# Wider dummy matmuls, fewer of them, and another order of the work

## The chip, the cores and the metric

The kernel runs on one core of a Trainium2 chip. A core has engines that each work through a queue of their own, in order: TensorE (PE in the profile; its weight loads are listed apart as PEld), VectorE (DVE), ScalarE (ACT), GpSimd (POOL) and SyncE (SP), which here only issues transfers. SBUF is the core's working memory; matmuls write to PSUM, here eight banks of 128 x 512 floats. The metric is the device time of one execution in microseconds (us), as a median over several runs.

## The reference

Eight sequences of 448 tokens with 12 heads of 64 go through an attention whose queries and keys are normalised, and then through a feed-forward layer of 768 to 2048 to 768 with a hard swish. There is no causal mask.

```python
def rmsnorm(x, g):
    return x / sqrt(mean(x * x, axis=-1) + 1e-6) * g
# q, k, v: (8, 12, 448, 64)
q_n, k_n = rmsnorm(q, g_q), rmsnorm(k, g_k)
scores = (q_n @ k_n.T) / sqrt(64)
attn = softmax(scores) @ v
x = attn.transpose(0, 2, 1, 3).reshape(3584, 768)
h = x @ w_in                      # (3584, 2048)
g = h * clip(h + 3, 0, 6) / 6
out = g @ w_out                   # (3584, 768)
```

## The kernel before

**Units of work.** Two heads of one sequence make a pair P; there are 48 pairs, six to a sequence (a batch b). For each pair SyncE loads q, k and v (256 KB each). The squares of q and k are taken on GpSimd or ScalarE (`square`, lines 357 to 361), summed over 64 on VectorE (L446, L480), and turned into inverse roots by a logarithm and an exponential on ScalarE (`roots`, L422 and L425). GpSimd or VectorE scales q and k by these to bf16 (`scale`, L364), and a cast brings v to bf16 beside a column of ones (`values`, by `copy`, L343 to L349). Pairs under 13 are transposed by TensorE into PSUM (L534) and copied out; later pairs by a transfer on SyncE's queue (L553), with a scaling behind it (L561, L563).

**Scores and weighted sums.** TensorE takes the scores of 112 keys against all 448 queries for both heads (L586, two matmuls that use 64 rows of the array each); ScalarE makes their exponentials (L592). The exponentials are the stationary operand of the weighted sums over v (L672), where the column of ones gives the sum for the softmax; VectorE divides (L688, L691). The result is transposed to xT by TensorE in batches 0 and 1 (L707, copied out), later by SyncE (L698).

**Feed-forward.** For each batch, 16 groups of hidden units: six matmuls of 448 columns into a PSUM bank (L764), then a clipped ReLU on ScalarE (L723) and one multiplication on VectorE (L726). For two batches together, 7 tiles of output rows: twice 16 matmuls of 384 columns (L786), copies out of PSUM on ScalarE or VectorE (L345, L347), stores. Two to five banks take turns. w_in and w_out come in four chunks each; GpSimd issues these transfers (L817, L822) between its own work, and they cast to bf16 under way.

**The first batch** is cut finer, so that TensorE can begin early: the queries are taken in two halves z of 224. `half_square` and `half_scale` treat half a pair's queries, `score_first` (L609, exponentials L614) and `av_first` (L631) work on one half, `finish_first` divides (L644, L647) and transposes (L656), and `h_first` (L745) runs hidden groups of batch 0 in two halves. Several of its tiles lie in the space of gT and xT, and so the profile names them gT or xT. Chunk 1 of w_in is first needed by hidden groups 2 and 3 of batch 0.

**Dummy matmuls** multiply a tile of zeros, zero_t. Their results are never used. `warm` (L377) makes 8 groups at the beginning and 22 between the first pieces of work, each group four matmuls of 128 columns. `idle` (L370) puts two matmuls of 64 columns ahead of each weighted sum of the first half z = 0, from pair 2 on, which is 16 times.

**What sets the order.** Nothing is decided while the kernel runs. `Plan.add` collects 2386 entries with their dependences, each an instruction or a few; `Plan.emit` writes them out in the order of the list `ORDER`, and a table `WAY` says by an entry's number which of its possible engines it goes to (0, the first one, where it isn't listed). `em` binds the instructions of an engine to this order. On TensorE that is 989 entries, on ScalarE 535, on VectorE 396, on SyncE 272, on GpSimd 194.

Of the kernel before, what the change touches and what calls it, by code (L numbers as in the profile page):

```python
# [203 lines left out]
def kernel(  # L204
# [59 lines left out]
    junk_t = const.tile([128, 1], FP32, name="junk_t")  # L264
    gr_t = const.tile([1, 2, D], FP32, name="gr_t")
    g8_t = const.tile([1, 2, D], FP32, name="g8_t")
    zero_t = const.tile([128, 128], BF16, name="zero_t")
    ones_t = const.tile([1, 1], FP32, name="ones_t")


# [349 lines left out]
    def av_first(P, z, t):  # L620
# [4 lines left out]
        def f_av(_):  # L625
            if P > 1 or z:
                idle(2 - 2 * z, X0_r[x])
# [326 lines left out]
```

## Time and profile before

| what | value |
|---|---|
| median of 3 runs | 427.37 us (426.27 to 429.7) |
| the profiled execution | 427.26 us |
| its span, first to last instruction | 425.2 us |
| granted TensorE clock over the span | 1.000 |
| GpSimd's work ends | near 330 us |

The rows in the text are of three kinds. A row of groups reads: line, engine, operation, tile written <- tiles read, shape, number of instructions | busy time, mean ns of one | idle time of the engine just before them and what ended it. A row of the timeline: start, length, engine, line, operation, and in brackets the idle time ahead of it. A row of waits: engine and line that waited <- engine and line waited for: us in total, times, longest. "issue" stands for a time in which no other engine's work is seen to have been waited for. Matmuls are pipelined: the record of one is longer than its step to the next, so that records overlap, and steps are read from starts.

### The profile page before, as it was taken

How to read it: one execution, taken by the hardware profiler on the slowest of the kernel's cores; microseconds unless marked ns; L12 is line 12 of the kernel's file. 1: busy time of each engine (PE TensorE's matmuls, PEld its weight loads, DVE VectorE, ACT ScalarE, POOL GpSimd, SP SyncE). 2: the span in 40 equal slices, each digit the busy share in tenths (PEclk: the TensorE clock that was granted, in tenths of full speed). 3: DMA queues.
4: the chain of work that ended last, by engine and by line, in shares of the span. 5: the costliest groups of instructions: out<-in, count | busy, mean ns of one | idle time of the engine just before them, and what ended most of it. 6: DMA issues, size and time to landing. Idle time of an engine off the chain costs nothing.

```text
span 425.2 us, 10132 instructions
## 1 busy us (share of the span) xinstructions
PE 415.3 (98%) x4050; PEld 248.5 (58%) x4050; DVE 220.6 (52%) x438; ACT 292.1 (69%) x533; POOL 179.9 (42%) x205
## 2 busy tenths in 40 slices
PE   7899999999999999999999999999999999999996
PEld 6665887554555555555555565555555555655564
DVE  5878777447965664545454555464434432233300
ACT  6899887789998886796867766587865842143211
POOL 4899777685876544446061472223410300000000
PEclk9999999999999999999999999999999999999999
DMA  7999999979969978665765348928530412101214
GB/s 252 295 270 257 225 237 179 298 196 238 246 158 215 243 197 206 158 178 146 164 184 168 69 108 184 239 64 212 124 75 11 113 49 67 49 2 47 66 40 145
DMA packets 98930, 67.76 MB, mean 159 GB/s; under 512 B 53156, under 2 KB 95428, under 8 KB 98884
## 3 DMA queue, kind: packets, MB, share of 16 engines
q1 hardware_dynamic: 93248, 60.50, 55.2%
q0 software_dynamic: 5248, 6.29, 8.9%
q8 instruction: 31, 0.51, 0.5%
q10 hardware_dynamic: 388, 0.34, 0.3%
q14 instruction: 15, 0.12, 0.1%
HBM read 50.23 MB, written 11.01 MB: 144 GB/s over the span
## 4 chain that ended last, share of the span: by engine, by line
PE 79%; DMA 8%; ACT 4%; DVE 3%; POOL 2%; issue 2%; SPq 1%; DVEq 0%; ACTq 0%; POOLq 0%
PE M L786 26%; PE M L764 24%; PE X L672 8%; PE S L586 5%; PE S L786 5%; PE M L745 4%; PE X L586 2%; DMA w_in_sb<-in_moe_w_in_dram 2%; ACT eT L614 2%; DMA gT<-in_q_dram 2%; DMA T<-qks 2%; PE X L764 1%; DMA qk<-in_k_dram 1%; POOL sq L361 1%; PE S L764 1%
## 5 line engine op out<-in xcount | busy, mean ns | idle before, releaser
L786 PE MATMUL M<-w_out_sb,gT 128*128 128x384 bf16 x752 | 137.8, 326 | 0.0
L364 POOL TENSOR_TENSOR qks<-qk,rs 112x512 bf16<-112x512 f32 (+1 forms) x90 | 91.5, 1030 | 104.2 <-ACT rs L425 57.9
L764 PE MATMUL M<-xT,w_in_sb 128*128 128x448 bf16 x618 | 134.4, 353 | 0.4 <-ACT y L345 0.2
L726 DVE SCALAR_TENSOR_TENSOR gT<-ts,M 128x448 bf16<-128x448 f32 x119 | 73.1, 617 | 90.4 <-ACT ts L723 89.4
L786 PEld LDWEIGHTS <-gT 128*128 128x128 bf16 x912 | 84.2, 98 | 57.7 <-issue 7.2
L592 ACT ACTIVATE eT<-S 112x896 bf16<-112x896 f32 x112 | 100.0, 916 | 7.7 <-PE S L586 5.0
L764 PEld LDWEIGHTS <-w_in_sb 128*128 128x128 bf16 x672 | 60.3, 98 | 57.8 <-issue 11.7
L723 ACT ACTIVATE ts<-M 128x448 f32<-128x448 f32 x119 | 64.6, 544 | 40.1 <-PE M L764 29.6
L361 POOL TENSOR_TENSOR sq<-qk 112x512 f32<-112x512 f32 (+1 forms) x60 | 60.7, 1019 | 40.0 <-DVE ssq L446 12.4
L592 ACT ACTIVATE eT<-X 112x896 bf16<-112x896 f32 x56 | 51.4, 918 | 17.6 <-PE X L586 16.8
L672 PEld LDWEIGHTS <-eT 112*128 112x128 bf16 x1344 | 53.2, 97 | 15.7 <-issue 2.2
L672 PE MATMUL X<-va,eT 112*128 112x65 bf16 x1344 | 56.8, 194 | 0.0
L446 DVE TENSOR_REDUCE ssq<-sq 112x16 f32<-112x1024 f32 x42 | 50.8, 1213 | 10.5 <-POOL sq L361 7.3
L586 PE MATMUL S<-T 64*128 64x448 bf16 x224 | 35.6, 353 | 0.0
L345 ACT COPY y<-M 128x384 f32<-128x384 f32 x28 | 13.4, 479 | 28.9 <-PE M L786 24.5
L691 DVE TENSOR_TENSOR xn<-X,rd 112x512 bf16<-112x512 f32 x42 | 28.9, 689 | 1.1
L586 PEld LDWEIGHTS <-T 64*128 64x128 bf16 x336 | 12.6, 94 | 24.4 <-issue 18.5
L745 PE MATMUL M<-xT,w_in_sb 128*128 128x224 bf16 x192 | 23.1, 259 | 0.6 <-DMA w_in_sb<-in_moe_w_in_dram 0.3
L347 DVE COPY y<-M 128x384 f32<-128x384 f32 x19 | 10.5, 554 | 25.2 <-PE M L786 21.5
L359 ACT ACTIVATE sq<-qk 112x512 f32<-112x512 f32 (+1 forms) x37 | 21.5, 590 | 2.6 <-DMA qk<-in_k_dram 2.2
L688 DVE RECIPROCAL rd<-X 112x8 f32<-112x8 f32 x42 | 8.6, 205 | 28.0 <-PE X L672 25.1
L786 PE MATMUL S<-w_out_sb,gT 128*128 128x384 bf16 (+1 forms) x128 | 22.9, 316 | 0.0
(84 smaller groups left out, 303.5 us busy)
## 6 DMA issues: line engine op xcount, KB each, us to landing
qk<-in_k_dram SPq DMA_DIRECT2D x45, 256.0 KB, 3.8
qk<-in_q_dram SPq DMA_DIRECT2D x45, 256.0 KB, 4.2
vf<-in_v_dram SPq DMA_DIRECT2D x45, 256.0 KB, 4.0
w_in_sb<-in_moe_w_in_dram POOLq DMA_DIRECT2D x4, 768.0 KB, 8.8
w_out_sb<-in_moe_w_out_dram POOLq DMA_DIRECT2D x4, 768.0 KB, 8.8
out_dram<-y SPq DMA_DIRECT2D x7, 336.0 KB, 3.9
out_dram<-y SPq DMA_DIRECT2D x8, 288.0 KB, 3.2
out_dram<-y SPq DMA_DIRECT2D x8, 240.0 KB, 3.6
```

Of the source, the lines that this page charges most:

```text
L361: em(nc.gpsimd.tensor_tensor(out=out, in0=in_, in1=in_, op=A_MULT))
L364: em((nc.vector if e == DVE else nc.gpsimd).tensor_tensor(out=out, in0=in_, in1=by.unsqueeze(3).to_broadcast(list(in_.shape)), op=A_MULT))
L446: em(nc.vector.tensor_reduce(out=ssq[:].rearrange("p i n -> p (i n)"), in_=sq[:].rearrange("p i (n d) -> p (i n) d", d=D), axis=AX_X, op=A ...
L586: em(nc.tensor.matmul(out=ps[:, a, 0:S], lhsT=qkT[r, S + t * TP:S + t * TP + 128], rhs=qkT[r, 0:S], start=True, stop=True))
L592: em(nc.scalar.activation(out=eT[:, t, 0:S2].rearrange("p (a s) -> p a s", a=2), in_=ps[0:TP, :, 0:S], func=EXP, bias=0.0, scale=1.0))
L672: em(nc.tensor.matmul(out=X_ps[:, a, i * E1:(i + 1) * E1], lhsT=eT[:, t, c:c + 128], rhs=va[:, a, t, :], start=(t == 0 and i == 0), stop=( ...
L691: em(nc.vector.tensor_tensor(out=xn[:].rearrange("p i a d -> p a i d"), in0=view()[:, :, :, 0:D], in1=rd[:].unsqueeze(3).to_broadcast([TP, ...
L723: em(nc.scalar.activation(out=ts[:], in_=ps()[:, 0:S], func=RELU, bias=0.5, scale=1.0 / 6.0))
L726: em(nc.vector.scalar_tensor_tensor(out=out, in0=shape(ts[:]), scalar=1.0, in1=shape(ps()[:, 0:S]), op0=A_MIN, op1=A_MULT))
L745: em(nc.tensor.matmul(out=ps()[:, f * SH:(f + 1) * SH], lhsT=w_in_sb[:, kt, f0:f0 + 128], rhs=xT[:, kt, z * SH:(z + 1) * SH], start=(kt == ...
L764: em(nc.tensor.matmul(out=ps()[:, 0:S], lhsT=w_in_sb[:, kt, f * 128:(f + 1) * 128], rhs=xT[:, kt, :], start=(kt == 0), stop=(kt == NKT - 1)))
L786: em(nc.tensor.matmul(out=ps()[:, 0:nc0], lhsT=gT[:, f, i * 128:(i + 1) * 128], rhs=w_out_sb[:, f, c0:c0 + nc0], start=(f == 0), stop=(f = ...
```

## The change

zero_t grows from 128 to 512 columns. A group of `warm` is one matmul with 512 moving columns instead of four with 128; `idle` is called for one matmul of 64 columns instead of two. Nothing else is added to the work or taken from it.

`ORDER` and `WAY` are new lists. Of the 2386 entries 106 go to another engine: among them 34 squares between ScalarE and GpSimd, 30 casts of v between three engines, 15 copies of outputs and 12 scalings of transposed keys between ScalarE and VectorE. In the first batch VectorE takes over the scaling of k4 (entry 126), the half scaling of q5 (154), the casts of v4 (128) and v5 (155) from GpSimd and two copies (241, 326) from ScalarE; GpSimd takes the casts of v1 (78) from VectorE and two half squares (230, 250) from ScalarE; ScalarE takes the cast of v3 (101) from VectorE and a half square (122) from GpSimd. The cast of v6 (346) goes from ScalarE to VectorE. On GpSimd's queue w_in chunk 3 (entry 3) moves next to chunk 2. VectorE has 409 entries after it, ScalarE 530, GpSimd 186.

```diff
 WAY = {
-    53: 1, 63: 2, 68: 1, 69: 1, 78: 2, 83: 1, 84: 1, 95: 1, 100: 1, 101: 2, 121: 1, 127: 1, 148: 1, 212: 1,
-    214: 1, 230: 1, 232: 1, 241: 1, 250: 1, 326: 1, 346: 1, 366: 2, 386: 1, 387: 1, 496: 2, 525: 1, 544: 1,
...
+    53: 1, 63: 2, 68: 1, 69: 1, 83: 1, 84: 1, 95: 1, 100: 1, 101: 1, 121: 1, 122: 1, 126: 1, 127: 1, 128: 2,
+    148: 1, 154: 1, 155: 2, 212: 1, 214: 1, 232: 1, 346: 2, 386: 1, 387: 1, 393: 2, 457: 1, 474: 1, 481: 1,
...
 ORDER = [
-    9, 20, 8, 21, 22, 11, 23, 10, 24, 25, 13, 28, 26, 14, 27, 53, 17, 31, 55, 32, 16, 33, 54, 212, 12, 34,
...
+    9, 20, 8, 21, 22, 11, 23, 10, 24, 25, 14, 28, 26, 13, 27, 53, 17, 31, 55, 32, 16, 33, 54, 56, 92, 34,
...
-    zero_t = const.tile([128, 128], BF16, name="zero_t")
+    zero_t = const.tile([128, 512], BF16, name="zero_t")
...
             em(nc.tensor.matmul(
-                out=ps[:, S:512], lhsT=zero_t[:], rhs=zero_t[:, 0:512 - S], start=False, stop=True,
+                out=ps[:, S:512], lhsT=zero_t[:, 0:128], rhs=zero_t[:, 0:512 - S], start=False, stop=True,
                 skip_group_check=True))
...
             for _ in range(n):
-                em(nc.tensor.matmul(out=ps, lhsT=zero_t[:], rhs=zero_t[:], start=True, stop=True))
+                em(nc.tensor.matmul(out=ps, lhsT=zero_t[:, 0:128], rhs=zero_t[:], start=True, stop=True))
...
             if P > 1 or z:
-                idle(2 - 2 * z, X0_r[x])
+                idle(1 - z, X0_r[x])
...
-        warm(S_r[1][:, 0, 0:128], ("S", 1), 4, "warm0")
+        warm(S_r[1][:, 0], ("S", 1), 1, "warm0")
...
-        warm(X0_r[1][:, 0:128], ("X", 1), 4, "warm1")
+        warm(X0_r[1][:], ("X", 1), 1, "warm1")
```

232 rows, old and new, of tables (ORDER, WAY) are left out of this document.

## The prediction

> **What bounds the kernel now.** I read the page's first part and then the same busy times by stage, because one share for the whole span mixes stages with different limits. A row by stage has the stretch, its length, busy us (and instructions) of TensorE, its weight loads, VectorE, ScalarE and GpSimd, the granted clock, the share and the rate of DMA.
>
> ```profile
> span 425.2 us, 10132 instructions
> ...
> PE 415.3 (98%) x4050; PEld 248.5 (58%) x4050; DVE 220.6 (52%) x438; ACT 292.1 (69%) x533; POOL 179.9 (42%) x205
> ```
>
> ```profile
> 15.00:20.00 5.00, 3.87 (x77) 3.06 (x75) 3.92 (x9) 4.84 (x13) 3.56 (x5) 1.00 1.00 278
> 20.00:41.00 21.00, 19.84 (x337) 13.29 (x333) 17.39 (x55) 20.46 (x38) 19.87 (x25) 1.00 1.08 263
> ...
> 60.00:410.00 350.00, 349.60 (x3143) 199.12 (x3142) 174.54 (x316) 236.24 (x420) 130.92 (x138) 1.00 0.60 144
> ```
>
> There are two regimes. From 60 to 410 us TensorE records 349.60 of 350 us: nothing but its own stream counts there. From 20 to 41 us ScalarE is the full engine (20.46 of 21.00) with GpSimd just behind (19.87); VectorE has 3.6 us free. [...] So a gain must come from (a) a shorter start, up to the point where TensorE is saturated, or (b) a shorter TensorE stream after it. Where the start ends, the chain of waits and the waits say:
>
> ```profile
> 32.35 8.92 DMA w_in_sb<-in_moe_w_in_dram
> 41.32 0.75 PE M L745 x6
> ```
>
> ```profile
> ACT sq L359 <- DMA gT<-in_k_dram: 0.7, 1, 0.7
> ACT eT L614 <- PE S L609: 0.4, 1, 0.4
> POOL qks L364 <- POOL sq L361: 0.5, 1, 0.5
> PE X L586 <- DVE xT L347: 0.4, 1, 0.4
> PE M L745 <- DMA w_in_sb<-in_moe_w_in_dram: 0.3, 1, 0.3
> ```
>
> TensorE goes over to steady work at 41.3 us, when the second chunk of w_in lands: issued by GpSimd at 32.35, 8.92 us under way. But the chunk is late by only 0.3 us; the wait of 0.4 just before it is for VectorE's copies of the last transposes of batch 0, and these hang on the exponentials. Three queues end nearly together here, so the gain of the start is that of the slowest of them.
>
> **The dummies.** They go from four 128-column matmuls to one of 512, thirty times, and from two 64-column ones to one, sixteen times.
>
> ```profile
> 11.40 0.84 PE L377 MATMUL XF<-zero_t 128*128 128x128 bf16 x12
> ...
> 13.37 0.39 PE L377 MATMUL XF<-zero_t 128*128 128x128 bf16 x4
> ...
> 16.53 0.37 PE L609 MATMUL S<-gT 64*128 64x224 bf16 x4 [1.11 <-ACT eT L614]
> ...
> 22.96 0.22 PE L370 MATMUL XF<-zero_t 128*128 128x64 bf16 x2
> ...
> 23.02 0.28 PE L631 MATMUL XF<-gT,eT 112*128 112x65 bf16 x4
> ```
>
> Twelve take 0.84 us and four 0.39, so one costs (0.84 - 0.39) / 8 = 0.056 us and a group of four 0.225. A matmul of 512 columns isn't seen; 448 columns take 0.19 (worked out below), the four 0.225. Between these I take 0.22, 448's share for 512. The difference is 0.1 us over 22 groups, 0.8 at the lower end, and they fill a TensorE that waits (1.11 us at 16.53): 0. If their cover went, they would cost what they cost now. Of the 64-column dummies two take 23.02 - 22.96 = 0.06 us, so 16 fewer are 0.5 us of TensorE between 16 and 29 us. ScalarE is full then and hides it; bounds 0 to -0.5, I take 0. The wider zero tile makes its clearing longer, unseen here at that width; its readers are dummies alone: 0, and a few tenths if a wait for loads did not cover it (0.77 at 3.61, shown below).
>
> **The start: what changes queue.** I counted, in each engine's order of both kernels, what stands ahead of the same late point. Prices:
>
> ```profile
> L359 ACT ACTIVATE sq<-gT 112x256 f32<-112x256 f32 x1 | 0.4, 407 | 0.0
> L345 ACT CAST va<-xT 112x512 bf16<-112x512 f32 x1 | 0.6, 617 | 0.0
> L345 ACT COPY xT<-XF 128x224 bf16<-128x224 bf16 x1 | 0.4, 367 | 0.0
> L345 ACT COPY gT<-M 128x224 bf16<-128x224 bf16 x1 | 0.3, 338 | 0.0
> ```
>
> ```profile
> 3.61 1.11 ACT L359 ACTIVATE sq<-qk 112x512 f32<-112x512 f32 x2 [0.77 <-DMA qk<-in_k_dram]
> ...
> 40.52 0.92 ACT L592 ACTIVATE eT<-X 112x896 bf16<-112x896 f32 x1
> ```
>
> ```profile
> L364 POOL TENSOR_TENSOR qks<-gT,rs 112x512 bf16<-112x512 f32 x3 | 3.1, 1047 | 0.6 <-POOL sq L361 0.5
> L361 POOL TENSOR_TENSOR sq<-qk 112x256 f32<-112x256 f32 x2 | 1.2, 612 | 0.0
> ...
> L349 POOL CAST gT<-vf 112x512 bf16<-112x512 f32 x2 | 1.2, 610 | 0.0
> ```
>
> ```profile
> L347 DVE COPY xT<-XF 128x224 bf16<-128x224 bf16 x11 | 2.8, 270 | 1.9 <-PE XF L656 1.9
> ...
> L343 DVE TENSOR_SCALAR_CACHE_REDUCE gT<-vf 112x512 bf16<-112x512 f32 x3 | 2.0, 683 | 0.0
> ...
> L364 DVE TENSOR_TENSOR qks<-qk,rs 112x256 bf16<-112x256 f32 x2 | 0.9, 455 | 0.0
> ```
>
> ```profile
> 39.60 0.46 DVE L347 COPY xT<-XF 128x224 bf16<-128x224 bf16 x2 [0.37 <-PE XF L656]
> ```
>
> *ScalarE*, up to the last exponential of pair 6 (40.52 + 0.92 = 41.44): it loses two half squares (2 x 0.41), a half transpose copy (0.34), an xT copy (0.37) and the cast of v6 (0.62), together 2.15; it gains a half square (0.41) and the cast of v3 (0.62): net -1.1. Two changes of place: the square of k5 now stands behind exponentials, so its 0.7 us wait for the load is filled; the half square of q0 moves from second place (the second of the two at 3.61, when ScalarE still waits for loads) to just ahead of the first exponential, +0.4. The two stand against each other up to 0.3, and the 0.4 us wait for scores may stay: -0.3 to -1.8, middle -1.1.
>
> *GpSimd*, up to the issue of w_in chunk 1: out go a half square, two casts and a half scaling (4 x 0.61) and the scaling of k4 (1.05), in come two half squares and a cast (3 x 0.61): -1.7. The scaling of q6 right ahead of the issue waits 0.5 us for the roots of pair 6; these move ahead of one exponential (0.92, the row above) on ScalarE. So the chunk can come 0.9 to 1.7 us earlier. Chunk 0 goes behind a cast of v1, about 0.6 us later; its first reader moves several instructions back on TensorE. Chunk 3 moves up next to chunk 2 and shares its bandwidth; chunk 2's readers come behind chunk 1's on TensorE. The loads keep their number ahead of every needed place but change order on SyncE's queue (k5 from 13th to 15th, q6 from 14th to 19th); q6's square stands 23rd on GpSimd's queue, k5's wait is counted above.
>
> *VectorE*, up to the same transposes' copies, takes what they give away: the scaling of k4, a half scaling, casts of v4 and v5, two copies, less the casts of v1 and v3. A full scaling is not seen on it: between 0.46 (the half) and 1.05 (GpSimd's full); I take 0.8, nearer to the half, twice of which is 0.9. The casts cancel (0.68 each): 0.8 + 0.46 + 2 x 0.27 = 1.8. It has 3.6 us free in 20 to 41, but not all in the right place: 0 to +1.8.
>
> So the handover moves by between -1.1 and +1.8 us; it cannot gain more than the tightest queue. I take -0.7: most of ScalarE's and GpSimd's shares, with some lost to VectorE.
>
> **The stream: what a switch to scores costs.**
>
> ```profile
> 133.93 1.30 PE L764 MATMUL M<-xT,w_in_sb 128*128 128x448 bf16 x6
> 135.44 0.73 PE L764 MATMUL M<-xT,w_in_sb 128*128 128x448 bf16 x3 [0.21 <-ACT y L345]
> ```
>
> ```profile
> 210.18 1.11 PE L764 MATMUL M<-xT,w_in_sb 128*128 128x448 bf16 x5
> 211.22 0.36 PE L586 MATMUL S<-T 64*128 64x448 bf16 x2
> 211.42 0.35 PE L586 MATMUL X<-T 64*128 64x448 bf16 x2
> 211.61 0.35 PE L586 MATMUL S<-T 64*128 64x448 bf16 x2
> 211.90 1.31 PE L786 MATMUL M<-w_out_sb,gT 128*128 128x384 bf16 x7
> ```
>
> ```profile
> PEld L586 <- issue: 18.5, 56, 0.4
> PEld L764 <- issue: 11.7, 35, 0.5
> PEld L786 <- issue: 7.2, 21, 0.4
> ```
>
> A step of 448 columns is (1.30 - 0.35) / 5 = 0.19 us (0.35 is one matmul's record). Five from 210.18 end at 211.13, but the scores start at 211.22: 0.10 late. Score pairs follow each other at 0.19 to 0.20; the last should be over at 211.80, and the next matmul starts at 211.90: 0.10 late again. So each run of scores, however long, costs 0.19 us. The weight loads show the same on both sides: 56 waits before scores, 35 + 21 = 56 behind them. Counted in the two orders, the 168 score groups after the first batch stand in 72 runs before and 67 after: 5 x 0.19 = -1.0 us, on the engine that sets the end; bounds -0.9 to -1.0, as a run that falls into the start counts nothing. [...]
>
> Stalls that remain: the two rows at 133.93 are one, 135.44 - 133.93 - 6 x 0.19 = 0.37 us, the largest beyond 60 us, for a bank that ScalarE had not emptied. Such stalls, by distances of starts, are 1.1 us beyond 60 and 1.4 between 41 and 60. The new order can lose them or bring others; bounds -2.5 to +2.5, I take 0: in both orders the matmul work between a hidden group and the next use of its bank is alike (a quarter of them have less than 1.7 us of it, added up from such steps). From 313 us on TensorE, ScalarE and VectorE run the same entries in the same order, so the end is as before.
>
> **Sum**, against the profiled execution's 427.26 us (span 425.2 and 2.1 around it; the median of the runs is 427.37, so the two stand for each other): -0.7 for the start, -1.0 for the switches, 0 for dummies and stalls: **425.6 us**.
>
> **Rivals.**
> 1. *Everything lands.* The start gains the 1.1 that GpSimd and ScalarE can both give, the 64-column dummies add 0.2 (7 of the 16 places on the path), the switches 1.0, and most stalls go (2.0): 427.3 - 4.3 = 423.0. For it speaks that all queues before 41 us are eased but one; against it, that stalls rarely all go.
> 2. *The change doesn't do what it says:* the start is no shorter, as the chunk, the copies and the exponentials trade places, and dummies were hidden anyway. Only the switches remain: 426.3.
> 3. *VectorE becomes the bound of the start*, slower than before. The 1.8 us given to it delay the copies of the last transposes, at 39.6 to 40.1 us, in full, and behind them the wide scores and the handover. 427.3 + 1.8 - 1.0 = 428.1. It decides once those copies come over 1.0 us later than now, which is what the five runs save; the 3.6 free us and the eased ScalarE ahead of it speak against, the 1.9 us that it waits for TensorE's transposes, a place where no work of its own fits, for it.
> 4. *The clock falls.* With fewer dummies TensorE idles more near 16 us and between 20 and 28. The granted clock is 1.00 in every stretch above, with an idle time of 1.11 us at 16.53, and 16 dummies fewer lengthen idle times by 0.03 us each. If a stretch of 5 us ran at half speed, it would cost between nothing and 5 us; I take 2.5, less the 1.0: 428.8. [...]
>
> **How the numbers follow.** Chances: forecast 0.55 (424.6 to 426.2), everything lands 0.15, switches alone 0.14, VectorE 0.12, clock 0.04. The range reaches from the first rival, a little beyond, to the third's: 422.7 to 429.0; it leaves out the clock's worse half, the worst of the stall bounds and half of the edge cases. A change below 1% (4.3 us) can hardly be told from none on this kernel. Faster by over 1%, below 423.1, needs all of the first rival: 0.09. Slower by over 1%, above 431.6, needs stalls or the clock at their upper bounds: 0.06. Within 1%: 0.85.
>
> **What would show it.** 3944 matmul records in place of 4050. The waits before scores fall from 56 to about 51. The first matmul on w_in chunk 1 starts near 40.6 instead of 41.3, with the chunk issued near 31.3. VectorE's busy time from 20 to 41 us is above 17.4 of 21, GpSimd's below 19.9. The granted clock stays at 1.00. I am wrong if VectorE becomes the releaser of TensorE's waits before 41 us, if a stall of over 0.5 us appears beyond 60, or if chunk 1 is issued no earlier.

## The result and the profile after

The changed kernel takes 426.38 us (median of 22 runs, 423.98 to 430.13), the kernel before beside it 428.16 (22 runs, 426.27 to 430.37): a ratio of 0.996, 95% interval 0.9943 to 0.9976, or 1.7 us less. On the 427.37 us from which the prediction started that is 425.7; forecast were 425.6. The profiled execution after took 424.44 us, 2.8 less than that of before, so it shows more than the medians do. Which part of it is typical is the main question below.

Lines moved by two: L379 are the wide dummies, L588 the scores, L616 the first batch's exponentials, L747, L766 and L788 the three feed-forward matmuls, L728 the gate. First the page's busy times, then the stretches, with the same columns as before.

```profile
PE 414.4 (98%) x3943; PEld 244.0 (58%) x3944; DVE 228.1 (54%) x459; ACT 289.2 (68%) x528; POOL 173.6 (41%) x197
```

```profile
15.00:20.00 5.00, 4.60 (x69) 2.86 (x66) 4.75 (x13) 4.88 (x15) 3.96 (x6) 1.00 1.11 315
20.00:41.00 21.00, 20.21 (x324) 13.88 (x323) 18.51 (x56) 20.50 (x34) 19.52 (x24) 1.00 1.10 242
...
60.00:410.00 350.00, 348.90 (x3127) 198.59 (x3125) 180.68 (x332) 232.30 (x412) 124.37 (x129) 1.00 0.61 144
```

VectorE has taken 1.1 us more work between 20 and 41 us (18.51 for 17.39), GpSimd 0.35 less, ScalarE is as full as before; the clock stands at 1.00. TensorE's 20.21 is no limit there: the record of a matmul of 448 columns lasts 0.35 us, its step to the next 0.19. Beyond 60 us TensorE has open places now (348.90 for 349.60), and VectorE's work there has grown from 174.54 to 180.68. The chain of waits at the end of the start, TensorE's timeline there, and the weight loads that waited for no other engine (us in total, times, longest):

```profile
37.13 1.73 ACT eT L594 x2
```

```profile
39.10 0.74 PE L747 MATMUL M<-xT,w_in_sb 128*128 128x224 bf16 x6
```

```profile
PEld L588 <- issue: 17.2, 53, 0.4
PEld L766 <- issue: 12.2, 37, 0.6
PEld L788 <- issue: 8.2, 24, 0.4
```

The first matmul on w_in chunk 1 starts at 39.10 us instead of 41.32, and no transfer stands in the chain ahead of it: two exponentials do. The waits ahead of scores fell from 56 to 53. These waits were not in the profile before; they stand in TensorE's timeline, with VectorE's beside it (start, length, work, in brackets the idle time ahead):

```profile
72.48 0.81 PE L788 MATMUL M<-w_out_sb,gT 128*128 128x384 bf16 x4 [0.16 <-DMA w_out_sb<-in_moe_w_out_dram]
92.82 1.93 PE L766 MATMUL M<-xT,w_in_sb 128*128 128x448 bf16 x9 [0.30 <-DVE y L349]
98.73 1.11 PE L766 MATMUL M<-xT,w_in_sb 128*128 128x448 bf16 x5 [0.53 <-DVE gT L728]
```

```profile
91.09 1.22 DVE L448 TENSOR_REDUCE ssq<-sq 112x16 f32<-112x1024 f32 x1
92.22 0.55 DVE L349 COPY y<-M 128x384 f32<-128x384 f32 x1
...
96.33 1.22 DVE L448 TENSOR_REDUCE ssq<-sq 112x16 f32<-112x1024 f32 x1 [0.98 <-POOL sq L363]
97.47 0.68 DVE L345 TENSOR_SCALAR_CACHE_REDUCE va<-vf 112x512 bf16<-112x512 f32 x1
...
98.07 0.62 DVE L728 SCALAR_TENSOR_TENSOR gT<-ts,M 128x448 bf16<-128x448 f32 x1
```

At 92 us a copy of y that frees a bank stands behind a reduction of 1.22 us; at 98 us a gate stands behind another reduction and a cast of v that was GpSimd's before. That reduction itself began late: VectorE had stood idle for 0.98 us until GpSimd's square was there. VectorE's work from 90 to 100 us (the third busy time in a row) before and after:

```profile
90.00:100.00 10.00, 9.94 (x102) 5.64 (x100) 5.33 (x11) 9.26 (x18) 6.43 (x8) 1.00 0.86 206
```

```profile
90.00:100.00 10.00, 9.17 (x106) 5.25 (x106) 8.27 (x17) 8.19 (x16) 8.89 (x10) 1.00 0.80 210
```

It is much busier there, 8.27 us for 5.33, but not full.

I took the start of every matmul of both traces and split the distance to the next into the matmul's own step (0.19 us for 448 columns, and so on), up to 0.1 us at each change to or from scores, and the rest as a wait. Between the two profiled executions the last matmul ends 2.56 us earlier (421.81 to 419.25): 2.22 us is the earlier handover to steady work, of which 0.19 goes back because two short matmuls on chunk 0 now stand behind it; 0.98 are score runs, of which there are 58 beyond 60 us where there were 63 (12.27 to 11.29 us); 0.4 are given back as waits behind the handover (1.79 to 2.22, each of over 0.02 us). Beyond 60 us alone the waits grow from 1.15 to 2.10; before 60 they shrink.

### The profile page after: what moved, and what is told of

The parts are those of the page before. It is cut to its first block, busy times and chain, and to the rows that moved or that the text cites. A ratio compares the mean times of both kernels' runs of the same rounds, so it can differ in the third digit from the quotient of the medians.

```text
span 422.6 us, 9945 instructions
## 1 busy us (share of the span) xinstructions
PE 414.4 (98%) x3943; PEld 244.0 (58%) x3944; DVE 228.1 (54%) x459; ACT 289.2 (68%) x528; POOL 173.6 (41%) x197
## 4 chain that ended last, share of the span: by engine, by line
PE 79%; DMA 8%; ACT 5%; POOL 3%; DVE 2%; issue 2%; SPq 1%; POOLq 0%; ACTq 0%
PE M L788 27%; PE M L766 26%; PE X L674 8%; PE S L588 5%; PE S L788 5%; DMA w_out_sb<-in_moe_w_out_dram 3%; PE X L588 2%; ACT eT L616 2%; PE M L747 2%; ACT eT L594 2%; DMA gT<-in_k_dram 1%; POOL qks L366 1%; PE X L766 1%; DMA qk<-in_k_dram 1%; DMA T<-qks 1%
## 5 line engine op out<-in xcount | busy, mean ns | idle before, releaser
L788 PE MATMUL M<-w_out_sb,gT 128*128 128x384 bf16 x752 | 139.5, 326 | 0.2 <-DMA w_out_sb<-in_moe_w_out_dram 0.2
L766 PE MATMUL M<-xT,w_in_sb 128*128 128x448 bf16 x618 | 134.8, 353 | 0.9 <-DVE gT L728 0.5
L366 POOL TENSOR_TENSOR qks<-qk,rs 112x512 bf16<-112x512 f32 (+1 forms) x89 | 90.5, 1031 | 82.5 <-ACT rs L427 51.3
L728 DVE SCALAR_TENSOR_TENSOR gT<-ts,M 128x448 bf16<-128x448 f32 x119 | 73.4, 618 | 83.7 <-ACT ts L725 83.2
L788 PEld LDWEIGHTS <-gT 128*128 128x128 bf16 x912 | 84.1, 98 | 59.1 <-issue 8.2
L766 PEld LDWEIGHTS <-w_in_sb 128*128 128x128 bf16 x672 | 60.3, 98 | 57.9 <-issue 12.2
L363 POOL TENSOR_TENSOR sq<-qk 112x512 f32<-112x512 f32 (+1 forms) x56 | 56.7, 1018 | 56.0 <-DMA qk<-in_q_dram 41.3
L588 PE MATMUL S<-T 64*128 64x448 bf16 x224 | 34.3, 353 | 0.0
L349 DVE COPY y<-M 128x384 f32<-128x384 f32 x26 | 14.4, 553 | 31.0 <-PE M L788 28.0
L588 PEld LDWEIGHTS <-T 64*128 64x128 bf16 x336 | 12.9, 94 | 24.3 <-issue 17.2
L361 ACT ACTIVATE sq<-qk 112x512 f32<-112x512 f32 (+1 forms) x41 | 23.8, 590 | 2.6 <-DMA qk<-in_k_dram 2.4
L347 ACT COPY y<-M 128x384 f32<-128x384 f32 x21 | 10.0, 478 | 22.5 <-PE M L788 18.4
L747 PE MATMUL M<-xT,w_in_sb 128*128 128x224 bf16 x192 | 23.0, 259 | 0.0
L788 PE MATMUL S<-w_out_sb,gT 128*128 128x384 bf16 (+1 forms) x128 | 23.0, 316 | 0.0
```

The costliest lines, as they stand in the source:

```text
L363: em(nc.gpsimd.tensor_tensor(out=out, in0=in_, in1=in_, op=A_MULT))
L366: em((nc.vector if e == DVE else nc.gpsimd).tensor_tensor(out=out, in0=in_, in1=by.unsqueeze(3).to_broadcast(list(in_.shape)), op=A_MULT))
L588: em(nc.tensor.matmul(out=ps[:, a, 0:S], lhsT=qkT[r, S + t * TP:S + t * TP + 128], rhs=qkT[r, 0:S], start=True, stop=True))
L728: em(nc.vector.scalar_tensor_tensor(out=out, in0=shape(ts[:]), scalar=1.0, in1=shape(ps()[:, 0:S]), op0=A_MIN, op1=A_MULT))
L747: em(nc.tensor.matmul(out=ps()[:, f * SH:(f + 1) * SH], lhsT=w_in_sb[:, kt, f0:f0 + 128], rhs=xT[:, kt, z * SH:(z + 1) * SH], start=(kt == ...
L766: em(nc.tensor.matmul(out=ps()[:, 0:S], lhsT=w_in_sb[:, kt, f * 128:(f + 1) * 128], rhs=xT[:, kt, :], start=(kt == 0), stop=(kt == NKT - 1)))
```

## The experiments

All times are compared with the kernel before, run between them on the same chip. "Handover" is the start of the first matmul on chunk 1 in the one profiled execution. In the rows of the experiments a line stands five lower than in the changed kernel (in e1, e3 and e8 five lower than in the kernel before): L742 is L747 there, L583 is L588.

| kernel | order and engines | dummies | median, us | ratio and interval | handover, us |
|---|---|---|---|---|---|
| before | before | before | 427.2 to 428.2 | 1 | 41.32 |
| changed | changed | changed | 426.38 | 0.9960 [0.9943, 0.9976] | 39.10 |
| e1_dummies | before | changed | 426.66 | 0.9983 [0.9963, 1.0003] | 40.62 |
| e2_lists | changed | before | 425.29 | 0.9934 [0.9911, 0.9956] | 39.29 |
| e3_new_start | changed up to the handover | changed | 426.39 | 0.9980 [0.9964, 0.9996] | 40.36 |
| e4_new_rest | changed from the handover on | changed | 426.51 | 0.9996 [0.9969, 1.0023] | 40.20 |
| e5_chunk_early | changed, chunk 1 earlier | changed | 425.71 | 0.9971 [0.9949, 0.9993] | 39.39 |
| e6_dve_order | changed, 3 entries moved | changed | 425.29 | 0.9950 [0.9930, 0.9971] | 39.05 |
| e7_split_runs | changed, 20 score runs more | changed | 431.71 | 1.0105 [1.0069, 1.0141] | 40.21 |
| e8_exps_first | before, 1 entry moved | before | 427.94 | 1.0009 [0.9989, 1.0029] | 40.84 |
| e9_no_idle | changed | no 64-column ones | 425.86 | 0.9952 [0.9926, 0.9979] | 41.42 |
| e10_no_warm | changed | second group 2 wide | 425.96 | 0.9970 [0.9944, 0.9997] | 40.52 |
| e11_old_dummies_dve | changed, 4 entries moved | before | 425.93 | 0.9956 [0.9935, 0.9977] | 39.86 |
| e12_fewer_runs | as e11, 3 score runs fewer | before | 428.31 | 1.0009 [0.9980, 1.0038] | 39.12 |

### Dummies or lists

The change taken apart in two: the new dummies in the old order, and the old dummies in the new order.

```diff
 # e1_dummies, against the kernel before
-    zero_t = const.tile([128, 128], BF16, name="zero_t")
+    zero_t = const.tile([128, 512], BF16, name="zero_t")
-                idle(2 - 2 * z, X0_r[x])
+                idle(1 - z, X0_r[x])
-        warm(X0_r[1][:, 0:128], ("X", 1), 4, "warm1")
+        warm(X0_r[1][:], ("X", 1), 1, "warm1")
 # e2_lists, against the kernel before: only ORDER and WAY of the changed kernel
```

> The order and engines of before with the new dummies alone. Theory (lists do it: an earlier handover to steady work by about 1.8 us, and five score runs fewer): the dummies stand beside waits and beside a full ScalarE, so the time is that of before within 0.6 us, and the handover stays near 41.3 us. Rival (the dummies do it: fewer TensorE microseconds in the start): 1.2 to 1.8 us less than before, handover near 40 us.

> The new order and engines with the old dummies (four of 128, two of 64). Theory: as fast as the changed kernel, 1.3 to 2.3 us less than before, handover near 39.5 us. Rival (dummies): the time of before within 0.6 us.

The lists alone give 0.66% less, 2.8 us, more than the 1.3 to 2.3 expected. The dummies alone give 0.17%, 0.7 us, with an interval that reaches 1: just over the 0.6 that the theory allowed and short of the rival's 1.2. Their handover came at 40.62, where 41.3 was expected. In the chain of e1_dummies the handover stands behind chunk 1 of w_in:

```profile
31.01 9.57 DMA w_in_sb<-in_moe_w_in_dram
```

The chunk was issued 1.3 us earlier than in the profile of before, and it would be easy to credit the dummies. But there is one visible difference ahead of it: in the old order ScalarE's square of k5 stands ahead of the exponentials of pair 2, and in the kernel before it waited 0.7 us for its load. In e1_dummies that load came in time, and the square ran at 13.99 us without a wait. Whether this moved the issue is doubtful: e8_exps_first below takes that wait out, and its chunk is issued only 0.23 us earlier. One profiled execution can't tell luck with a load from an effect of the dummies.

### The start alone and the rest alone

The lists were cut at the first matmul on chunk 1: e3_new_start has the new lists up to it and the old ones for what is left, e4_new_rest the reverse. Both have the new dummies.

> New dummies; the new order and engines up to the first matmul on w_in chunk 1, the old order and engines for all that is left. 93 score runs, so nothing is saved on switches. Theory: the start alone is worth 1.5 to 2.0 us less than before, and the stalls at 72, 92 and 98 us of the changed kernel are not there. Rival (the switches carry the gain, the earlier handover is lost to later waits): the time of before within 0.5 us.

> New dummies; the old order and engines up to the first matmul on w_in chunk 1, the new ones for all that is left. 87 score runs. Theory: five switches less are 1.0, new stalls take back 0.4 to 1.0, so 0 to 0.6 us less than before, handover at 41.3 us. Rival (the start is worth nothing): 1.3 to 2.3 us less than before.

The new start is worth 0.2%, 0.9 us, between what the theory and its rival expected; the new rest by itself nothing that the timing shows, which is within what its theory allowed, although its trace has its 58 score runs beyond 60 us. Its handover of 40.20 with the old start, where 41.3 was expected, shows how far one execution differs from the next. The chain and TensorE's timeline of e3_new_start, then the timeline of e4_new_rest:

```profile
30.23 10.08 DMA w_in_sb<-in_moe_w_in_dram
```

```profile
40.36 0.84 PE L740 MATMUL M<-xT,w_in_sb 128*128 128x224 bf16 x7 [1.71 <-DMA w_in_sb<-in_moe_w_in_dram]
```

```profile
70.04 0.65 PE L783 MATMUL M<-w_out_sb,gT 128*128 128x384 bf16 x3 [0.60 <-DMA w_out_sb<-in_moe_w_out_dram]
...
164.38 0.55 PE L583 MATMUL S<-T 64*128 64x448 bf16 x4 [0.64 <-ACT eT L589]
165.63 0.37 PE L583 MATMUL X<-T 64*128 64x448 bf16 x2 [0.69 <-ACT eT L589]
```

In e3_new_start the chunk was issued 2.1 us earlier than before, but took 10.08 us instead of 8.92, and TensorE waited 1.71 us for it. So a start that runs ahead can lose its gain to the transfer. In e4_new_rest w_out (issued closer together in the new order) is waited for, and two runs of scores wait for ScalarE: more than the five runs save. The old order is not free of such waits either: e1_dummies waits 0.91 us at 89.51 and e3_new_start 1.05 us at 89.59 for a quotient of VectorE, and e8_exps_first 0.36 and 0.41 us at 70 and 74 us for w_out. In the profile before none of them is there.

### Is it the landing of chunk 1?

e5_chunk_early issues chunk 1 two GpSimd passes earlier. e8_exps_first tests the other wait, that for k5's load, alone in the old order. The diffs from here on name entries of the lists, with their numbers in brackets: sq is a square, sc a scaling, e an exponential, red2 a reduction, cy a copy of y, cv a cast of v, kt a scaling of transposed keys, rd a reciprocal; s is a tile of scores, h and y are parts of hidden and output groups.

```diff
 # e5_chunk_early: GpSimd's entries in the changed ORDER
-    sq q7 (359), sc q6 (344), w_in 1 (1), sc k6 (345)
+    w_in 1 (1), sq q7 (359), sc q6 (344), sc k6 (345)
 # e8_exps_first: ScalarE's entries in ORDER of before
-    sq k5 (148), e P2z0c0 (157), e P2z0c1 (159)
+    e P2z0c0 (157), e P2z0c1 (159), sq k5 (148)
```

> The changed kernel with one GpSimd entry moved: the transfer of chunk 1 of w_in is issued ahead of the square of q7 and the scaling of q6, about 28.8 us instead of 30.84. Theory (the end of the start hangs on this chunk, whose transfer took 7.9 us in one profile and 10.1 in another): the chunk lands before 38.9 in any case, no wait for it is left ahead of the first matmul that reads it, and the time falls by 0.3 to 0.9 us against the changed kernel, to a ratio of about 0.994 against the kernel before. Rival (the chunk is not late in the typical execution): the two GpSimd passes are 0.9 us later and q6's transposes with them, and the time is the changed kernel's or up to 0.9 us more, ratio 0.996 to 0.998.

> The kernel before with one ScalarE entry moved: the square of k5, which waited 0.71 us at 15.04 us for its load, goes behind the two exponentials of pair 2 that stood behind it. Theory (that wait is one of the terms that the new order takes out of the start): the exponentials of pair 2 start 1.2 us earlier, the chain of the start is 0.7 us shorter, and the time falls by 0.4 to 0.8 us, ratio 0.998 to 0.999. Rival (the start ends with the landing of chunk 1 of w_in, and GpSimd's queue sets that): the first matmul on the chunk starts within 0.3 us of 41.3 as before, ratio 1.000.

Neither theory holds as a time, though in e5_chunk_early the chunk landed before 38.9 and was not waited for, as expected. The issue of chunk 1 with the time to its landing (the last number) in the changed kernel, and the same with GpSimd's timeline, the chain and TensorE's timeline in e5_chunk_early:

```profile
w_in_sb<-in_moe_w_in_dram POOLq DMA_DIRECT2D x1, 768.0 KB, 7.8
```

```profile
w_in_sb<-in_moe_w_in_dram POOLq DMA_DIRECT2D x1, 768.0 KB, 10.4
```

```profile
28.40 0.88 POOL L814 DMA_DIRECT2D w_in_sb<-in_moe_w_in_dram  x1
```

```profile
37.42 1.74 ACT eT L589 x2
```

```profile
39.39 0.74 PE L742 MATMUL M<-xT,w_in_sb 128*128 128x224 bf16 x6
```

Issued at 30.84, the chunk of the changed kernel landed at 30.84 + 7.8 = 38.6 us; issued at 28.40, 2.4 us earlier, it landed at 28.40 + 10.4 = 38.8. In this pair the transfer took up the whole lead. The changed kernel's DMA share is 1.11 and 1.10 in the two stretches shown from 15 to 41 us, and from 30.5 to 32 us the queue of the loads alone has 107.1%, which fits a chunk that has to share with the loads. But one profile of each doesn't show that the earlier issue made the transfer longer: issued at 30.22 and 30.23, the chunk took 8.85 us in e12_fewer_runs and 10.08 in e3_new_start. And the exponentials set the handover at 39.39, as they did at 39.10: in both profiles the chunk was there half a microsecond ahead.

ScalarE's timeline and the chain of e8_exps_first:

```profile
14.63 1.73 ACT L609 ACTIVATE eT<-S 112x896 bf16<-112x896 f32 x2
```

```profile
32.12 8.68 DMA w_in_sb<-in_moe_w_in_dram
40.84 0.75 PE M L740 x6
```

In e8_exps_first the exponentials start 0.95 us earlier than before (14.63 for 15.58), but the chunk's issue moves only from 32.35 to 32.12, and the handover hangs on that. GpSimd's queue, not ScalarE's, issues the chunk; easing ScalarE alone did not bring it forward by much.

### What VectorE's late waits cost

e6_dve_order takes the three waits of the profile after out by their order; e11_old_dummies_dve mends what that left and has the old dummies.

```diff
 # e6_dve_order, against the changed kernel: VectorE, then GpSimd
-    red2 P19 (855), cy g0i2n0 (481)
+    cy g0i2n0 (481), red2 P19 (855)
-    cv P17 (802), gate b1f3 (688)
+    gate b1f3 (688), cv P17 (802)
-    w_out 2 (6), sc k11, ..., cv P9, w_out 3 (7)
+    w_out 2 (6), w_out 3 (7), sc k11, ...
 # e11_old_dummies_dve: besides, with the dummies of before
-    red2 P19 (855), kt P16, rd P13, gate b1f1 (680)
+    gate b1f1 (680), red2 P19 (855), kt P16, rd P13
```

> The changed kernel with three entries moved: on VectorE the copy of y ahead of the reduction for pair 19, the gate of the fourth tile of batch 1 ahead of the cast of V of pair 17, and on GpSimd the last chunk of w_out right behind the third. Theory (the three stalls of 0.32, 0.47 and 0.69 us at 72, 92 and 98 us are VectorE's overload and a late chunk, and come every time): all three go, the time falls by 0.7 to 1.5 us, ratio 0.993 to 0.994 against the kernel before. Rival (these waits change from execution to execution, or the work behind them is late next): within 0.4 us of the changed kernel, ratio 0.995 to 0.997.

> The order and engines of the changed kernel with the dummies of the kernel before, and four entries moved: on VectorE the copy of y and then the gate of the second tile of batch 1 ahead of the reduction for pair 19, the gate of the fourth tile ahead of the cast of V of pair 17, on GpSimd the last chunk of w_out right behind the third. Theory (the gate's wait of 0.82 us at 94 us in the run with the copy alone moved was the reduction put ahead of it, and with both ahead nothing is late next): no stall over 0.3 us between 90 and 100 us, and 0.5 to 1.0 us less than the same lists without these moves, ratio 0.991 to 0.993. Rival (VectorE's load in that stretch is what counts, and its order only moves the wait on): another stall of 0.4 us or more between 90 and 105 us, ratio 0.993 to 0.995.

Against the changed kernel e6_dve_order is no different that can be measured (0.995 and 0.996), nor e11_old_dummies_dve against the same lists unmoved (0.9956 and 0.9934). The last is above both ranges that were expected of it. Timeline of TensorE and VectorE in e6_dve_order, then of TensorE in e11_old_dummies_dve:

```profile
95.02 0.73 PE L761 MATMUL M<-xT,w_in_sb 128*128 128x448 bf16 x3 [0.82 <-DVE gT L723]
```

```profile
92.08 0.56 DVE L344 COPY y<-M 128x384 f32<-128x384 f32 x1 [0.48 <-PE M L783]
92.56 1.21 DVE L443 TENSOR_REDUCE ssq<-sq 112x16 f32<-112x1024 f32 x1
```

```profile
95.55 0.55 PE L583 MATMUL S<-T 64*128 64x448 bf16 x4 [0.19 <-DVE T L560]
96.39 0.37 PE L583 MATMUL X<-T 64*128 64x448 bf16 x2 [0.29 <-DVE xn L688]
```

With the copy ahead, the gate behind the same reduction is late by 0.82 us; with the gate ahead too, the scaling of transposed keys and the quotient are, by 0.19 and 0.29. The wait moves from one product of VectorE to the next, as the rival has it, but in e11_old_dummies_dve it also shrinks, below the 0.4 us that the rival named. That VectorE's load is the cause and not its order isn't shown: in e6_dve_order the copy that was put ahead kept VectorE idle for 0.48 us until TensorE had written its bank, and the reduction started that much later. A kernel with less work for VectorE in this stretch wasn't run. The wait for w_out at 70 to 72 us is gone in both, and that too shows in no median.

### What a run of scores costs

```diff
 # e7_split_runs, against the changed kernel, in 20 places from 128 to 246 us
-    s P21t1, s P21t3, h b2f3.0, h b2f3.1
+    s P21t1, h b2f3.0, s P21t3, h b2f3.1
 # e12_fewer_runs, against e11_old_dummies_dve, at 142, 161 and 310 us
-    s P21t2, s P23t1, y g0i4n1.0, y g0i4n1.1, s P22t3, s P22t1
+    y g0i4n1.0, y g0i4n1.1, s P21t2, s P23t1, s P22t3, s P22t1
```

> The changed kernel with 20 more runs of score matmuls between 128 and 246 us (108 for 88): in 20 places the last score tile of a run goes behind the next part of h or y; no instruction is added. Theory (each run costs 0.19 us in its two changes of shape): 3.8 us more than the changed kernel, ratio 1.005 to the kernel before. Rival (the change of shape costs nothing of its own, and the time between shapes is put there by something else): no slower than the changed kernel by more than 0.5 us, ratio 0.996 to 0.997.

> The kernel of old_dummies_dve with three runs of scores fewer (85 for 88): at 142, 161 and 310 us the parts of h or y between two runs go ahead of the first. Theory (each run costs 0.18 us, as the 20 more runs showed in their changes of shape): 0.55 us less, ratio about 0.001 below that of old_dummies_dve. Rival (the scores put off leave ScalarE late, and the wait comes back as a stall behind them): a new stall of 0.2 us or more within 4 us of one of the three places, and the time of old_dummies_dve or more.

Twenty runs more cost 1.0105 / 0.996 - 1 = 1.5%, 6.2 us, 0.31 each, where 3.8 us were expected. Weight loads of e7_split_runs that waited for no other engine, and TensorE's timeline at one of the places:

```profile
PEld L583 <- issue: 24.9, 75, 0.5
PEld L761 <- issue: 13.9, 47, 0.6
PEld L783 <- issue: 10.7, 36, 0.5
```

```profile
131.31 0.82 PE L783 MATMUL M<-w_out_sb,gT 128*128 128x384 bf16 x4
132.38 0.65 PE L669 MATMUL X<-va,eT 112*128 112x65 bf16 x16 [0.26 <-ACT eT L589]
```

Ahead of scores 22 waits were added (53 to 75) and behind them 22 (61 to 83). By the starts of the matmuls the changes of shape take 3.9 us more, 0.20 a run, as the prediction had it; the rest is mostly waits like that at 132.38, some 2 us between 128 and 250 us: a score put off by one part of h or y makes its exponential late for the weighted sum. The other way round it is worse, as the rival of e12_fewer_runs had it: with three runs fewer that kernel saves 0.6 us in changes of shape, and its median is 2.4 us above e11_old_dummies_dve:

```profile
143.26 0.36 PE L583 MATMUL X<-T 64*128 64x448 bf16 x2 [0.63 <-ACT eT L589]
...
163.11 0.55 PE L583 MATMUL S<-T 64*128 64x448 bf16 x4 [0.82 <-ACT eT L589]
164.35 0.36 PE L583 MATMUL X<-T 64*128 64x448 bf16 x2 [0.69 <-ACT eT L589]
...
313.69 0.36 PE L583 MATMUL X<-T 64*128 64x448 bf16 x2 [0.63 <-ACT eT L589]
```

Each joined run now waits for ScalarE to empty a bank that its last scores write, at exactly the three places, by 0.6 to 1.5 us. A run's 0.2 us is saved only where the exponentials of the joined scores are done by then.

### What the dummies are worth

```diff
 # e9_no_idle, against the changed kernel
-                idle(1 - z, X0_r[x])
+                idle(0, X0_r[x])
 # e10_no_warm: m is 512 where it isn't given
-                em(nc.tensor.matmul(out=ps, lhsT=zero_t[:, 0:128], rhs=zero_t[:], start=True, stop=True))
+                em(nc.tensor.matmul(out=ps[:, 0:m], lhsT=zero_t[:, 0:128], rhs=zero_t[:, 0:m], start=True, stop=True))
...
-        warm(X0_r[1][:], ("X", 1), 1, "warm1")
+        warm(X0_r[1][:], ("X", 1), 1, "warm1", 2)
```

> The changed kernel with all 16 remaining 64-column dummies beside the weighted sums left out; the dummies of 512 columns stay. This leaves out no part of the result. Theory (these dummies lie in TensorE's waits for ScalarE and cost nothing): the first matmul on w_in chunk 1 starts within 0.4 us of 39.3, clock 1.00, and the time is the changed kernel's within 0.4 us, ratio 0.995 to 0.997. First rival (they are on the chain: 16 of 28 ns beside the sums): 0.4 to 0.5 us less, ratio 0.995. Second rival (they keep the clock up): a granted clock below 1.00 between 15 and 41 us and the time up by 1 us or more, ratio 0.998 or above.

> The changed kernel with the second group of 512-column dummies (4.6 to 19 us) cut to 2 columns each, so that TensorE idles there; the first group and the 64-column dummies stay. This leaves out no part of the result. Theory (in the start ScalarE and the loads set the pace, and the dummies only keep the clock): if the granted clock stays 1.00 after 20 us, the time is the changed kernel's within 0.5 us, ratio 0.995 to 0.997; if it falls, the stage up to 41 us gets longer by its matmuls that lie on the chain, some 4 to 6 us of them at half the clock, ratio 1.005 to 1.010. Rival (the wide dummies delay the transposes and scores that come due behind them): the exponentials of pair 2 start 0.3 us or more earlier and the time falls by 0.3 to 0.8 us, ratio 0.994 to 0.995.

The chain of e9_no_idle, then a stretch and TensorE's timeline of e10_no_warm:

```profile
32.21 9.17 DMA w_in_sb<-in_moe_w_in_dram
```

```profile
15.00:20.00 5.00, 4.80 (x58) 3.06 (x58) 4.65 (x11) 4.72 (x11) 3.49 (x7) 0.50 1.10 320
```

```profile
40.52 0.74 PE L742 MATMUL M<-xT,w_in_sb 128*128 128x224 bf16 x6
```

With the second group of wide dummies cut down TensorE runs at half its clock from about 8 to 22 us in the profile, and yet the time is the changed kernel's (0.997 and 0.996), not the 1.005 to 1.010 expected for that case. The handover at 40.52 is 1.4 us later than in the changed kernel's profile, and 0.2 later than in any other profile of the new start but that of e9_no_idle. Without the 64-column ones the median is the changed kernel's as well. The handover of e9_no_idle, 41.42, is 2.3 us late against what was expected, behind a chunk that was issued at 32.21. Its granted clock from 15 to 41 us is 1.00, so that rival's sign is not there; what delayed this one execution isn't shown. The seven kernels that have the new lists whole or with a few entries moved for test, except those with other score runs, lie between 0.9934 and 0.9971, mean 0.9956: the two with the old dummies at 0.9934 and 0.9956, three with the new at 0.9960, 0.9971 and 0.9950, two with fewer at 0.9952 and 0.9970. Dummies sort them in no way that the intervals allow to be read.

No version is clearly ahead of both kernels: e2_lists has the lowest ratio, but its interval overlaps that of the changed kernel.

## Why the prediction was right, step by step

**Time and sign.** 0.996 of 427.37 is 425.7 us, beside 425.6. The sum holds with other terms: some -1.0 for the start (-0.7 forecast), -1.0 for the switches (as forecast), +0.4 for stalls (0) make -1.6, and the ratio stands for 1.7. The start and the stalls are known to a few tenths at best, so part of the hit is luck: two misses, of the start and of the stalls, offset each other.

**The start, -0.7.** In the two profiled executions the handover moved by -2.2, outside the bounds that the step gave (-1.1 to +1.8). The lower bound was too narrow by its own terms: it took the middle of ScalarE's share, where ScalarE's and GpSimd's own bounds (-1.8 and -1.7) allowed -1.7. Much of that is the choice of executions. The four kernels with the old start hand over at 40.20 to 41.32, mean 40.75; the eight with the new start and neither group of dummies cut down further at 39.05 to 40.36, mean 39.55, 1.2 us earlier; with e9_no_idle and e10_no_warm in, the mean is 39.83, 0.9 us earlier. e3_new_start, the new start alone, measures 0.2% of 427.7, 0.9 us. So the term is about -1.0, and undersized by some 0.3 us, about what I had VectorE take back. It did take on the work (18.51 of 21 us), but the longest wait of TensorE for it from 15 to 41 us is 0.3. That this is where the 0.3 us lie isn't shown.

The mechanism was right in its main point, three queues that end together, and the two experiments that eased one alone gained little: e8_exps_first for ScalarE, e5_chunk_early for the chunk. What I missed is how much the chunk's transfer varies, from 7.8 to 10.4 us in the profiles shown. It was taken as 8.92, whenever it is issued.

**The switches, -1.0.** Right: 63 runs to 58 beyond 60 us, -0.98 us in the distances. Of the price, 0.20 us a run is confirmed by e7_split_runs. That it is all a run costs is not: moving scores changes when exponentials end, and e12_fewer_runs lost 3.9 us in waits beyond 128 us against the 0.6 that it saved.

**Stalls, 0.** The weakest step. Its ground, that the matmul work between a hidden group and its bank's next use is alike, looked at one consumer. VectorE's load beyond 60 us, 6 us more, wasn't weighed, nor the four chunks of w_out issued closer together. The waits behind the handover grew by 0.4 us in the profiled pair, and the sign of failure that I had named, a stall of over 0.5 us beyond 60, is there at 98.73 (0.53). But both are weak evidence. Counted in the same way, the waits are 1.8 to 2.8 us in the three profiles with the old lists (mean 2.3) and 2.2 to 3.7 in the seven with the new ones, whole or with a few entries moved (mean 2.8); and the old order, too, has stalls of over 0.5 us in two of its profiles. So 0.4 to 0.5 us is what the profiles suggest, well inside the bounds, and a single stall was a poor sign. In the changed kernel's profile VectorE is the releaser of the two largest waits, at 92 and 98 us, and not, as the third rival had it, of one that holds up the start. That its load there is the cause is argued and not shown.

**Dummies, 0.** Right within 0.2 to 0.3%, which is all that these runs can tell: the new dummies are 0.17% faster than the old in the old order (e1_dummies) and 0.26% slower in the new one (e2_lists against the changed kernel), neither clear of the noise. The bound of -0.5 for the 64-column ones cannot be excluded.

**The clock.** 1.00 as forecast in the changed kernel's profile. But idle times of 1.11 us at full clock that grow by 0.03 each were too thin a reason: in e9_no_idle the clock fell to 0.50 with no idle time of over 1.41 us from 3 us up to the fall. And the price of 2.5 us for 5 us at half speed was too high: e10_no_warm spent 13.65 us at half speed in its profile, for at most 1.4 us there. The median shows nothing, though only seven of its twelve executions have the profile's granted clock of 0.98; their median is 426.3 us, that of the three at full clock 425.7. One profile of each kernel also hid that the clock is not the same in every execution: of 98 of the kernel before, timed beside the experiments, 18 show 0.996 or less, and their median is 429.3 us, against 427.2 for the others; so do 3 of the changed kernel's 22. At 0.996, if the fall was to the 0.50 of e10_no_warm, 3.4 of 425 us ran at half speed, by my estimate, while 13.65 us of it cost e10_no_warm little; so whether the fall costs those 2 us, or comes of the same waits that do, stays open. The gain of the lists doesn't hang on it: with the executions at 0.998 or more alone, e2_lists has 425.3 us and the kernel before beside it 427.3.

**What the signs said.** 3943 records for 3944 and 53 waits for about 51 fit; so do the chunk's issue (30.84 for 31.3), VectorE above 17.4 and GpSimd below 19.9. The handover, 39.10 for 40.6, doesn't fit; between the means of the two starts it moves by 0.9 to 1.2 us where 0.7 were named.

**What stays open.** Start and rest, each alone, give 0.2% and 0.04%, the whole lists between 0.3 and 0.7%. The intervals allow a plain sum at their edges. Whether the new rest needs the earlier start to keep clear of waits such as those at 164 us in e4_new_rest wasn't separated.

## What to carry to other kernels

Where several queues end together at a handover, price a change there by what all of them allow, and read the end of a transfer as a range over several profiles: the one traced pair here overstated the gain of the start by a microsecond, as much as that gain. Don't book an earlier issue of a transfer as an earlier end: in the one pair tried here, with the transfer engines full (107.1% from 30.5 to 32 us in the changed kernel, 81.7% and 21.4% by the two queues from 27 to 34.2 us in e5_chunk_early), 2.4 us at the issue were nothing at the landing. Take the start of a matmul from the timeline: a piece of the chain begins only where the piece ahead of it ends, here 0.17 us later. A switch cost that is read from starts of matmuls holds for counting, but an order with fewer switches is only cheaper if what the moved work frees is free in time; count the second consumer of each moved step, and the load of the engine that takes it over. If taking out a wait by order makes the next product of the same engine late, look at whether the engine stood idle ahead of it: only if it didn't is its load the likely cause.

## What the runs showed of the hardware

The granted clock fell without any single idle time of over 2.2 us. TensorE's timeline in e10_no_warm, with two stretches of it, the same of e9_no_idle, where the wide dummies remain, and a stretch of the kernel before:

```profile
6.54 0.37 PE L531 MATMUL M<-identity,qks 112*128 112x112 bf16 x4 [1.17 <-POOL qks L361]
9.07 0.37 PE L531 MATMUL M<-identity,qks 112*128 112x112 bf16 x2 [2.16 <-POOL qks L361]
```

```profile
4.72:8.13 3.41, 1.02 (x15) 0.73 (x13) 1.25 (x3) 1.46 (x5) 1.20 (x2) 1.00 0.98 300
...
8.00:20.00 12.00, 9.64 (x112) 6.58 (x113) 10.86 (x28) 11.58 (x32) 9.49 (x13) 0.51 1.10 342
```

```profile
8.22 0.27 PE L531 MATMUL M<-identity,qks 112*128 112x112 bf16 x2 [1.41 <-POOL qks L361]
...
10.82 0.37 PE L531 MATMUL M<-identity,qks 112*128 112x112 bf16 x2 [0.67 <-POOL qks L361]
```

```profile
7.29:10.70 3.41, 1.78 (x17) 0.87 (x17) 2.42 (x7) 2.67 (x11) 2.21 (x3) 1.00 1.04 357
...
11.00:12.00 1.00, 1.00 (x5) 0.44 (x4) 1.00 (x4) 1.00 (x5) 0.99 (x2) 0.50 1.11 352
```

```profile
7.17:10.58 3.41, 2.04 (x29) 1.48 (x28) 2.87 (x8) 2.94 (x11) 2.44 (x4) 1.00 1.05 362
```

In e10_no_warm TensorE did no more than four transposes in the 3.7 us up to 9.07 (1.17 + 0.37 + 2.16); in e9_no_idle its waits are 1.41 and 0.67 us. The clock falls to half within the wait of 2.16 us in the one and within that of 0.67 in the other. In e10_no_warm it is at half from 8.13 to 21.78 us, 13.65 us, and TensorE is recorded busy for 9.64 of the 12 us from 8 to 20; in e9_no_idle it is at half from 10.70 to 14.11, 3.41 us. In a stretch of these 3.41 us ahead of the fall TensorE is recorded busy for 1.02 us in e10_no_warm and 1.78 in e9_no_idle, 30% and 52%; in the kernel before a stretch as long with 2.04 us, 60%, was followed by full clock. What lowers the clock, and at what limit, these three traces don't show. And the half clock cost e10_no_warm at most the 1.4 us of its later handover: ScalarE is busy for 11.58 of those 12 us.
